# Threshold attention and a gelu feed-forward on one core: a planner whose ranks go down to single pairs and single weight pieces

## Chip, cores and metric

The kernel runs on one core of a Trainium2 chip. The metric is the device time of one execution in microseconds (us). The times given are medians of several runs.

## The reference

Two blocks follow each other. All arrays are fp32; q, k and v are 8 batches x 8 heads x 576 rows x 64, x is 4608 x 512, w_in is 512 x 2048 and w_out is 2048 x 512.

```python
def _attn_ref(q, k, v, tau):
    scale = 1.0 / np.sqrt(q.shape[-1])
    scores = scale * np.matmul(q, k.transpose(0, 1, 3, 2))
    thresh = np.max(scores, axis=-1, keepdims=True) - tau
    scores = np.where(scores >= thresh, scores, -1000000000.0)
    scores = scores - np.max(scores, axis=-1, keepdims=True)
    attn = np.exp(scores)
    attn = attn / (np.sum(attn, axis=-1, keepdims=True) + 1e-09)
    return np.matmul(attn, v)

# x = attention output, transposed to (batch * seq, heads * head_dim)
def _moe_ref(x, w_in, w_out):
    h = x @ w_in
    g = h * (1.0 / (1.0 + np.exp(-1.702 * h)))
    return g @ w_out
```

The host hands the weights over as 64-bit floats; the kernel turns them into fp32 itself.

## The kernel before

**Work.** Two heads of one batch are a *pair*: 32 pairs, four for each batch. Pairs 0 to 3 are one batch, and every four pairs complete 576 rows of x. The feed-forward block works on blocks of 256 rows; the first two blocks are computed together as soon as x of pairs 0 to 3 stands.

**One pair.** SP loads q, k and v. VectorE transposes q and k (`prep`, L522). TensorE multiplies 64x64 tiles (`scores`, L538), nine key tiles j for each pair, four matmuls each. ScalarE copies each result to SBUF (`keep`, L555); VectorE takes maxima in groups (`in_groups`, L561), over tiles (`over_tiles`, L570) and over halves (`over_halves`, L581 and L594). The maxima are transposed (`turn_rows`, L605), written to memory by SP (`row_out`, L651) and read back spread over the partitions (`row_in`, L660); pair 2 does this with a VectorE transpose instead (`spread_max`, L642). VectorE subtracts (`sub`, L666), five tiles t for each pair; ScalarE masks (`mask`, L672) and takes exponentials (`exps`, L676). TensorE multiplies by v (`values`, L687, tile pv). The sums of exponentials come from TensorE for pairs 0 to 4 (`sums_by_pe`, also L687, tile den, then `one_row`, L718 and L722, and `spread_sums`, L770 and L772), and from VectorE and a round trip through memory from pair 5 on (`turn_sums`, L744 to L749, `sums_out`, `sums_in`). `place_x` (L789) scales pv and writes it to xT.

**Weights.** There are 32 pieces, 16 of w_in and 16 of w_out. POOL issues two DMAs for each (`load_w`, L473 and L474), each piece after the one before it and when its slot is free: pieces go to one of four stages inside w_out or to one of two spare slots of the arena. A piece is converted by VectorE (`cv_ex` L484, `cv_frac` L498 and L502, `cv_end` L510) and ScalarE (`cv_power`, L492). `cv_end` frees the slot.

**Feed-forward.** For the first two blocks 16 hidden tiles are computed (`mm1_0`, L844, eight matmuls each), then tanh on ScalarE (L813) and a product on VectorE (`gelu_0`, L850), then the second matmul (`mm2`, L826) in eight groups of two weight rows for each of four row blocks. Later blocks use L804, L816 and seven-product sums (L995); the last four use L909 too. Hidden tiles use the PSUM pool psM of two banks; scores, pv and some others use psA of three slots.

**Order.** Nothing is ordered by the loops themselves. Each step becomes a *task* with an engine, a cost, a rank, the tasks that it comes after and the buffers that it takes and gives back. `run_in_order` then plays the tasks through an event loop: whenever an engine is free, the ready task with the lowest rank starts, and its instructions are issued. The program that runs on the chip holds each engine's instructions in the order so found. The rank of an attention task is the number of its pair plus a bias by kind of task:

```python
        if 0 <= rank < LAST:
            biases = EARLY if a[0] < NPAIR else SECOND if a[0] < 2 * NPAIR else LATER
            rank += CV[f.__name__] if f.__name__ in CV else biases.get(f.__name__, 0.0)
```

EARLY holds for pairs 0 to 3, SECOND for 4 to 7, LATER from 8 on, CV for the weight tasks. `W_RANK` gives six numbers from which the base rank of each weight piece is interpolated. Feed-forward matmuls have rank 1000 and most of their followers rank -9.

Of the kernel before, what the change touches and what calls it, by code (L numbers as in the profile page):

```python
# [30 lines left out]
def kernel(  # L31
# [97 lines left out]
    for x in ("raw0", "raw1", "qkT0", "qkT1", "mb"):  # L129
# [3 lines left out]


    EARLY = {
        "exps": -17.61,
        "in_groups": 12.77,
        "keep": 26.48,
        "load_qk": 6.42,
        "load_v": 0.46,  # L140
        "mask": 4.73,
        "one_group": -15.86,
        "one_row": -9.06,
        "over_halves": -11.42,
        "over_tiles": -0.06,
        "place_x": -9.61,
        "prep": -11.56,
        "row_in": 31.26,
        "row_out": -12.68,
        "scores_run": 26.41,  # L150
        "spread_max": 4.27,
        "spread_sums": 4.87,
        "sub": 8.56,
        "sums_by_pe": -5.69,
        "sums_in": 2.27,
        "sums_out": 16.51,
        "turn_rows": -16.86,
        "turn_sums": -5.4,
        "values": 24.67,
        "w_sum": 2.1,  # L160
        "x_sum": -20.63,
    }
    SECOND = {
        "exps": -12.92,
        "in_groups": 29.73,
        "keep": 6.19,
        "load_qk": 1.9,
        "load_v": 13.07,
        "mask": 1.29,
        "one_group": 2.55,  # L170
        "one_row": -2.79,
        "over_halves": -24.79,
        "over_tiles": 9.26,
        "place_x": -19.31,
        "prep": -22.42,
        "row_in": -9.56,
        "row_out": -26.33,
        "scores_run": 2.45,
        "spread_max": 6.39,
        "spread_sums": -1.67,  # L180
        "sub": 27.62,
        "sums_by_pe": 38.88,
        "sums_in": 16.9,
        "sums_out": 8.98,
        "turn_rows": 12.04,
        "turn_sums": -0.33,
        "values": 2.02,
        "w_sum": -3.88,
        "x_sum": -12.22,
    }  # L190
    LATER = {
        "exps": 1.49,
        "in_groups": 1.97,
        "keep": -9.78,
        "load_qk": -5.98,
        "load_v": -3.59,
        "mask": 21.95,
        "one_group": 4.78,
        "one_row": -20.84,
        "over_halves": 8.94,  # L200
        "over_tiles": -3.1,
        "place_x": 4.68,
        "prep": -7.1,
        "row_in": 2.23,
        "row_out": -2.52,
        "scores_run": -13.43,
        "spread_max": -3.68,
        "spread_sums": -27.9,
        "sub": 9.4,
        "sums_by_pe": 4.28,  # L210
        "sums_in": 8.55,
        "sums_out": -0.12,
        "turn_rows": -4.72,
        "turn_sums": 8.12,
        "values": 0.63,
        "w_sum": 21.55,
        "x_sum": 7.65,
    }
    CV = {
        "cv_end": -26.29,  # L220
        "cv_ex": 6.34,
        "cv_frac": -13.49,
        "cv_power": -9.91,
        "load_w": 3.03,
    }

    LAG = {"PE": 0.26, "DVE": 0.18, "ACT": 0.22, "POOL": 0.18, "SP": 0.1}
# [4 lines left out]
    def task(engine, cost, rank, f, *a, after=(), take=(), give=(), lag=None):  # L232
        if lag is None:
            lag = LAG[engine]
        if 0 <= rank < LAST:
            biases = EARLY if a[0] < NPAIR else SECOND if a[0] < 2 * NPAIR else LATER
            rank += CV[f.__name__] if f.__name__ in CV else biases.get(f.__name__, 0.0)
        tasks.append((engine, cost, rank, f, a, [x for x in after if x is not None],
                      take, give, lag))
        return len(tasks) - 1  # L240
# [9 lines left out]
    def transfer(by, time, a, kind=0, give=(), lag=1.7):  # L250
        return task(by, time, FIRST, moved, kind, after=[a], give=give, lag=lag)
# [144 lines left out]
    def own(n, *pools):  # L396
        return tuple(x + "_apart" for x in pools) if n in APART else pools
# [678 lines left out]
    FFU = 1.727  # L1076
    T_RANK = FIRST

    W_RANK = (0, 15.75, 22.55, 26.06, 2.06, 16.74)
    ready_w, w_loads, w64 = [], [], 0  # L1080
    for i in range(len(pieces)):
        y = 0 if i < NDC else 2 if i < n_in else 4
        n = NDC if i < NDC else n_in - NDC if i < n_in else n_in
        first = (0, 0, NDC, 0, n_in)[y]
        rank = W_RANK[y] + (W_RANK[y + 1] - W_RANK[y]) * (i - first) / n
        if not wide:
            ready_w.append(task("POOL", 1.2, rank, load_w, i, lag=2.5))
            continue
        x = stage(i)
        place = (f"w64_{w64 % 2}",) if x is None else (f"stage{x}",)  # L1090
        w64 += x is None
        a = task("POOL", 1.1, rank, load_w, i, after=w_loads[-1:], take=place)
        w_loads.append(a)
        a = transfer("DMW", 3.4, a)
        e = task("DVE", 0.34, rank, cv_ex, i, after=[a])
        m = task("ACT", 0.67, rank, cv_power, i, after=[e])
        a = task("DVE", 0.95 + SHARED, rank, cv_frac, i, after=[e])

        over = [ready_w[y] for y in range(i) if i >= n_in and stage(y) == (i - n_in) // PER_STAGE]
        ready_w.append(task("DVE", 0.61 + SHARED, rank, cv_end, i, after=[a, m] + over, give=place))  # L1100
# [191 lines left out]
    for n in range(NP):  # L1292
# [39 lines left out]
        if n >= JOINT:  # L1332

            a = None
            for t in range(NKT + 1):
# [11 lines left out]
                a = w  # L1347
                for j in js:
# [6 lines left out]
                    a = w  # L1355
                if t == NKT:
                    valued(m, w)
        else:
            for js in [range(x, x + 3) for x in range(0, NK, 3)] if n >= WHOLE else [[x] for x in range(NK)]:
                new = sum((own(n, "s_m") if x < NK - 1 else ("s_t",) for x in js if x % 2 == 0), ())  # L1360
                a = task(
                    "PE", 0.484 * slow * len(js), r, scores_run, n, js, after=[pq, pk] + after,
                    take=("psA",) * len(js) + new,
                    give=own(n, "qkT0", "qkT1") if js[-1] == NK - 1 and n not in TWICE else (),
                )
# [3 lines left out]
        a = task("DVE", 0.47, r, over_tiles, n, ALU.max, after=mx)  # L1369
        quick = n in BY_DMA or n in TWICE  # L1370
        a = task(
            "DVE", 1.05 if not quick else 1.3 if n in TWICE else 0.8, r, over_halves, n,
            after=[a, tau_done], take=("row",) if quick else (),
        )
        if n in TWICE:
            m = task("DVE", 0.6, r, row_blocks, n, after=[a], take=own(n, "mb"), give=("row",))
        elif n in BY_DMA:
            a = task("DVE", 0.21, r, turn_rows, n, after=[a])
            a = transfer("DMS", 0.3, task("SP", 0.65, r, row_out, n, after=[a]))
# [6 lines left out]
        for t in range(NKT + 1):  # L1386
            tail = t == NKT
            if n in TWICE:
                for j in range(2 * t, min(2 * t + 2, NK)):
# [4 lines left out]
                    a = task("ACT", 0.62, r, mask_one, n, j, after=[m] + mx, give=("psA",))  # L1394
# [3 lines left out]
            a = task(  # L1398
                "POOL" if pool else "DVE", (1.45 if pool else 0.68) if tail else 2.7 if pool else 1.3,
                r, sub, n, t, after=[y for y, x in subs if tail or x in (None, pool)],  # L1400
                give=own(n, "mb") if tail else (),
            )
            subs.append((a, pool))
            a = task("ACT", 0.7 if tail else 1.18, r, mask, n, t, after=[a])
# [4 lines left out]
        if n < NPAIR:  # L1409
# [15 lines left out]
            if n in SUMS_BY_PE:  # L1425
                a = task("DVE", 1.07, r, one_row, n, after=[den], give=("psM", "psM"))
            else:
                back += (v_m,)
        else:
# [3 lines left out]
            if n in SUMS_BY_PE:  # L1433
                a = task("PE", 4.36, r, sums_by_pe, n, every, False, after=ws + [pv], take=("psA",), give=back)
                if pv is None:
                    su = [a]
                a = task("DVE", 1.07, r, one_row, n, after=[a], give=("psA",))
        if n not in SUMS_BY_PE:
# [4 lines left out]
            a = task("DVE", 0.47, r, over_tiles, n, ALU.add, after=su + [pv], give=back)  # L1443
            if n in SUMS_BY_DMA:
                a = task("DVE", 1.46, r, turn_sums, n, after=[a], take=("row_s",))
                a = transfer("DMS", 0.3, task("SP", 0.65, r, sums_out, n, after=[a]))
                a = task("SP", 1.2, r, sums_in, n, after=[a], take=("rc",))
                summed[n] = transfer("DMS", 0.7, a, 1, give=("row_s",))
            else:
                a = task("DVE", 1.6, r, one_group, n, after=[a])  # L1450
# [41 lines left out]
```

## Time and profile before

| | |
|---|---|
| median of 3 runs | 1313.1 us (1312.97, 1313.1, 1314.63) |
| profiled execution, its own time | 1311.6 us |
| its span, first to last instruction | 1309.8 us |
| TensorE (PE) matmul busy | 1260.5 us, 96% |
| VectorE (DVE) busy | 1002.2 us, 77% |
| ScalarE (ACT) busy | 646.6 us, 49% |
| GpSimd (POOL) busy | 246.1 us, 19% |
| mean granted TensorE clock | 0.989 |

The profile is one execution, and its times are counted from the start of the span. In a row of the timeline the columns are start, length, engine, line, operation, what is written from what, and in brackets the idle time of the engine ahead of it and what ended that idle time. A row of the waits reads: who waited, for whom, us in total, number of times, longest. One fp32 matmul appears as two records, so the eight matmuls of a hidden tile are sixteen records. "PEld" is the loading of weights into TensorE.

### The profile page before, as it was taken

How to read it: one execution, taken by the hardware profiler on the slowest of the kernel's cores; microseconds unless marked ns; L12 is line 12 of the kernel's file. 1: busy time of each engine (PE TensorE's matmuls, PEld its weight loads, DVE VectorE, ACT ScalarE, POOL GpSimd, SP SyncE). 2: the span in 40 equal slices, each digit the busy share in tenths (PEclk: the TensorE clock that was granted, in tenths of full speed). 3: DMA queues.
4: the chain of work that ended last, by engine and by line, in shares of the span. 5: the costliest groups of instructions: out<-in, count | busy, mean ns of one | idle time of the engine just before them, and what ended most of it. 6: DMA issues, size and time to landing. Idle time of an engine off the chain costs nothing. (4 is left out here: it accounts for less than half of the span.)

```text
span 1309.8 us, 22824 instructions
## 1 busy us (share of the span) xinstructions
PE 1260.5 (96%) x9128; PEld 972.6 (74%) x9128; DVE 1002.2 (77%) x1601; ACT 646.6 (49%) x830; POOL 246.1 (19%) x300
## 2 busy tenths in 40 slices
PE   5869999999999999999999999999999999999998
PEld 2436854477688777777778888777777778888887
DVE  7999998989998877778877877777888864652642
ACT  5975656766664544455554545454556540210210
POOL 1301210022030212112020302020212117120120
PEclk8989999999999999999999999999999999999999
DMA  6976967264322222221222222222122110000000
GB/s 118 339 186 214 282 209 132 67 125 83 82 57 71 55 64 64 56 57 44 63 47 61 55 71 55 72 56 70 42 52 54 38 44 9 9 1 33 1 1 32
DMA packets 194309, 103.78 MB, mean 79 GB/s; under 512 B 160284, under 2 KB 171292, under 8 KB 194204
## 3 DMA queue, kind: packets, MB, share of 16 engines
q1 hardware_dynamic: 180476, 64.30, 20.6%
q0 software_dynamic: 11360, 37.74, 9.7%
q8 instruction: 71, 1.16, 0.4%
q10 hardware_dynamic: 2368, 0.30, 0.2%
q14 instruction: 34, 0.28, 0.1%
HBM read 88.40 MB, written 9.70 MB: 75 GB/s over the span
## 5 line engine op out<-in xcount | busy, mean ns | idle before, releaser
L561 DVE TRANSPOSE_TENSOR_REDUCE part<-arena 128x36 f32<-128x1152 f32 x295 | 361.5, 1241 | 45.9 <-ACT arena L555 32.3
L804 PE MATMUL hps<-xT,w_in 128*128 128x256 f32 x1536 | 336.9, 380 | 0.4 <-DVE arena L816 0.4
L804 PEld LDWEIGHTS hps<-xT,w_in 128*128 128x128 f32 x1536 | 290.8, 190 | 45.5 <-issue 5.7
L672 ACT ACTIVATE arena<-arena 128x1152 f32<-128x1152 f32 (+1 forms) x160 | 169.4, 1058 | 144.9 <-DVE arena L666 144.6
L555 ACT COPY arena<-ps 128x576 f32<-128x576 f32 x288 | 170.4, 647 | 121.2 <-PE ps L538 120.9
L666 DVE TENSOR_TENSOR arena<-arena 128x1152 f32<-128x1152 f32 (+1 forms) x158 | 197.5, 1281 | 19.6 <-DMA arena<-row 19.5
L995 PE MATMUL ops<-w_out,arena 128*128 128x256 f32 x896 | 202.9, 381 | 1.2 <-DVE arena L816 1.1
L676 ACT ACTIVATE arena<-arena,shift,scl 128x1152 f32<-128x1152 f32 (+1 forms) x160 | 200.1, 1251 | 4.1
L538 PE MATMUL ps<-arena 64*64 64x288 f32 x2304 | 174.1, 419 | 25.1 <-DVE arena L522 14.4
L995 PEld LDWEIGHTS ops<-w_out,arena 128*128 128x128 f32 x896 | 169.0, 190 | 29.1 <-DVE arena L816 3.7
L961 POOL TENSOR_TENSOR arena<-arena 128x256 f32<-128x256 f32 x56 | 50.8, 907 | 658.4 <-DVE arena L816 556.7
L687 PE MATMUL pv<-arena 64*64 64x288 f32 x2176 | 161.2, 410 | 0.0
L538 PEld LDWEIGHTS ps<-arena 64*64 64x64 f32 x2304 | 83.7, 137 | 93.6 <-ACT arena L555 30.7
L995 PE MATMUL ops<-arena 128*128 128x256 f32 x672 | 150.6, 380 | 0.0
L813 ACT ACTIVATE th<-hps 128x512 f32<-128x512 f32 x112 | 66.0, 589 | 167.9 <-PE hps L804 148.2
L995 PEld LDWEIGHTS ops<-arena 128*128 128x128 f32 x672 | 127.3, 190 | 19.3 <-issue 2.2
L687 PEld LDWEIGHTS pv<-arena 64*64 64x64 f32 x2176 | 82.0, 135 | 55.3 <-issue 12.8
L1017 DVE SCALAR_TENSOR_TENSOR osb<-ops,osb 128x256 f32<-128x256 f32 x98 | 39.5, 414 | 91.8 <-PE ops L995 85.0
L816 DVE SCALAR_TENSOR_TENSOR arena<-th,hps 128x512 f32<-128x512 f32 x96 | 64.1, 667 | 37.1 <-ACT th L813 37.0
L844 PE MATMUL hps<-xT,w_in 128*128 128x256 f32 x256 | 57.3, 382 | 1.3 <-DVE arena L850 1.2
L826 PE MATMUL ops<-w_out,arena 128*128 128x512 f32 x128 | 56.4, 596 | 0.0
L844 PEld LDWEIGHTS hps<-xT,w_in 128*128 128x128 f32 x256 | 48.1, 190 | 11.0 <-DVE arena L850 3.0
(117 smaller groups left out, 1027.8 us busy)
## 6 DMA issues: line engine op xcount, KB each, us to landing
arena<-in_v_dram SPq DMA_DIRECT2D x128, 144.0 KB
arena<-in_q_dram SPq DMA_DIRECT2D x128, 72.0 KB
out_dram<-osb SPq DMA_DIRECT2D x36, 256.0 KB
arena<-in_k_dram SPq DMA_DIRECT2D x124, 72.0 KB
arena<-row SPq DMA_DIRECT2D x62, 144.0 KB
arena<-row_s SPq DMA_DIRECT2D x54, 144.0 KB
w_out<-in_moe_w_in_dram POOLq DMA_DIRECT2D x12, 512.0 KB, 9.4
arena<-in_moe_w_out_dram POOLq DMA_DIRECT2D x12, 512.0 KB, 5.9
```

Of the source, the lines that this page charges most:

```text
L538: nc.tensor.matmul(ps[ts(c, KT), h, 0:SH], lhsT=mats[n, 1][ts(h, D), ts(j, KT)], rhs=mats[n, 0][ts(h, D), ts(c, SH)], start=True, stop=True,)
L555: nc.scalar.copy(out=sT[n, t][:, u], in_=pss.pop((n, j))[:, :, 0:SH])
L561: nc.vector.tensor_reduce(out=stats[n, op][:, t * 2 * QB : min(2 * t + 2, NK) * QB], in_=sT[n, t].rearrange("p u h (g d) -> p (u h g) d", ...
L666: engine.tensor_tensor(out=s, in0=s, in1=mbs[n].unsqueeze(1).to_broadcast(list(s.shape)), op=ALU.subtract)
L672: nc.scalar.activation(out=s, in_=s, func=AF.Prelu, alpha=STEEP)
L676: nc.scalar.activation(out=s, in_=s, func=AF.Exp, scale=scl, bias=shift)
L687: nc.tensor.matmul(o[c][ts(h, D), 0:SH], lhsT=left(j, h)[ts(c, KT)], rhs=sT[n, t][ts(c, KT), u, h, :], start=(j == 0), stop=(j == NK - 1),)
L804: nc.tensor.matmul(hidden[j][:, ts(f, BLK)], lhsT=w_in[:, c, ds((f * HF + j) * P, P)], rhs=xTs[blk][:, c, :], start=(c == 0), stop=(c == N ...
L813: nc.scalar.activation(out=ths[j], in_=hidden[j], func=AF.Tanh, scale=GELU_SCALE / 2)
L816: nc.vector.scalar_tensor_tensor(out=g[:, :, j, :], in0=two(ths.pop(j)), scalar=1.0, in1=two(hidden.pop(j)), op0=ALU.add, op1=ALU.mult,)
L844: nc.tensor.matmul(hidden[j][:, ts(i, BLK)], lhsT=w_in[:, c, ts(j, P)], rhs=xTs[i][:, c, :], start=(c == 0), stop=(c == NDC - 1),)
L995: nc.tensor.matmul(banks[blk][k][:, ts(o, HM)], lhsT=left[:, j, :], rhs=right[:, j, :], start=(j == 0), stop=(j == HF - 1),)
```

## The change

A table FINE is added: for each kind of task, a number for single pairs (0 to 11) or, for the weight tasks, single pieces (0 to 31). It is added to the rank on top of the bias by kind. All numbers of EARLY, SECOND, LATER, CV and W_RANK that have an effect are replaced as well. Costs, buffers, task lists and everything that a task computes are the same. Lines behind the table stand 31 to 32 further down in the changed file; this document uses the line numbers of the kernel before.

```diff
     EARLY = {
-        "exps": -17.61,
-        "in_groups": 12.77,
-        "keep": 26.48,
-        "load_qk": 6.42,
...
+        "exps": -15.19,
+        "in_groups": 17.23,
+        "keep": 16.21,
+        "load_qk": 18.68,
...
+    FINE = {
+        "cv_end": {0: -4.24, 1: 0.97, 2: -0.08, 3: 0.15, 4: -0.51, 5: -1.84, 6: 3.35, 7: -7.43, 9: -1.14,
...
+        "exps": {0: -2.59, 1: -0.69, 2: 6.36, 4: -3.4, 5: -2.14, 6: -1.95, 7: -3.02, 8: 0.63, 11: 0.04},
...
+        "scores_run": {1: 3.05, 2: -2.01, 3: -0.82, 4: 0.23, 6: 0.66, 7: -1.37, 8: -0.72, 9: -1.56, 11: -0.25},
...
+        "w_sum": {0: 3.24, 1: 2.7, 3: -1.58},
+    }
     CV = {
-        "cv_end": -26.29,
-        "cv_ex": 6.34,
-        "cv_frac": -13.49,
-        "cv_power": -9.91,
-        "load_w": 3.03,
+        "cv_end": -25.54,
+        "cv_ex": -1.8,
+        "cv_frac": 3.09,
+        "cv_power": -11.15,
+        "load_w": 15.66,
     }
...
             rank += CV[f.__name__] if f.__name__ in CV else biases.get(f.__name__, 0.0)
+            rank += FINE.get(f.__name__, {}).get(a[0], 0.0)
...
-    W_RANK = (0, 15.75, 22.55, 26.06, 2.06, 16.74)
+    W_RANK = (5.06, 3.62, 24.06, 7.16, 8.62, 12.37)
```

In the built program this moves instructions on TensorE, VectorE, ScalarE and SP. Up to the first feed-forward matmul, TensorE's list changes as follows: the score matmuls of pair 3 stand between the den and pv matmuls of pair 1 instead of behind them; those of pair 4 between the den and pv matmuls of pair 2; those of pair 5 between the den and pv matmuls of pair 3, with one tile of nine left behind them. In the list of L826, a run of 4 and 16 matmuls around the scores of pair 6 becomes 10 and 2, and the run between pair 5's and pair 6's `values` grows from 30 to 38. On VectorE, 10 weight pieces instead of 13 stand ahead of `place_x` of pair 3, in the order 0, 1, 2, 3, 9, 8, 6, 4, 5, 7 instead of ascending. On SP, half of the first v loads move behind the q and k loads that followed them.

## The prediction

> **What bounds the kernel now.** I read the page's totals first, then busy time by stretch, then TensorE's waits, then the timeline at the places that the waits name.
>
> ```profile
> PE 1260.5 (96%) x9128; PEld 972.6 (74%) x9128; DVE 1002.2 (77%) x1601; ACT 646.6 (49%) x830; POOL 246.1 (19%) x300
> ```
>
> The 96% is a mean over unlike stages. Stretches cut where the work changes (columns: stretch, length, then busy us of PE, PEld, DVE, ACT, POOL, granted clock, DMA share, GB/s):
>
> ```profile
> 20.00:114.00 94.00, 65.17 (x865) 36.07 (x865) 90.86 (x157) 74.52 (x90) 18.16 (x33) 0.87 0.78 231
> 114.00:165.00 51.00, 49.74 (x228) 42.14 (x230) 48.26 (x77) 27.33 (x36) 12.64 (x23) 1.00 0.79 252
> 165.00:246.00 81.00, 78.52 (x545) 40.11 (x544) 74.45 (x121) 54.52 (x64) 8.40 (x12) 1.00 0.64 153
> 246.00:420.00 174.00, 171.37 (x1328) 126.48 (x1329) 157.11 (x238) 104.83 (x134) 32.68 (x30) 0.99 0.38 82
> 420.00:1310.00 890.00, 884.59 (x6026) 723.10 (x6024) 620.14 (x991) 374.57 (x490) 171.47 (x184) 1.00 0.18 45
> ```
>
> Up to 114 us VectorE is full (90.86 of 94) and PE is not (65.17). From 114 to 246 both are nearly full. After 420 PE alone is full and VectorE has 270 us to spare. So the change, which reorders the first twelve pairs, can only save PE idle time ahead of about 420 us. PE's waits in the whole run:
>
> ```profile
> PE den L687 <- ACT arena L676: 16.5, 4, 6.8
> PE ps L538 <- DVE arena L522: 14.4, 3, 8.7
> PE ps L538 <- ACT arena L555: 6.4, 10, 2.4
> PE ps L538 <- DVE xT L789: 4.1, 3, 1.6
> PE hps L844 <- DVE arena L850: 1.2, 3, 0.8
> ```
>
> The first four are nearly all ahead of the first feed-forward matmul (L844, at 113.93). What is left after it: 1.2 on the gelus (L850), 4.9 of the 6.4 on score copies (L555), 1.5 on L816. Three places in the timeline of PE carry the argument:
>
> ```profile
> 110.27 3.73 PE L538 MATMUL ps<-arena 64*64 64x288 f32 x32 [1.64 <-DVE xT L789]
> ...
> 157.83 7.17 PE L844 MATMUL hps<-xT,w_in 128*128 128x256 f32 x32 [0.79 <-DVE arena L850]
> ...
> 246.30 1.43 PE L538 MATMUL ps<-arena 64*64 64x288 f32 x16 [2.44 <-ACT arena L555]
> ```
>
> Ahead of the third, on VectorE:
>
> ```profile
> 220.62 1.36 DVE L666 TENSOR_TENSOR arena<-arena 128x1152 f32<-128x1152 f32 x1 [0.91 <-DMA arena<-row]
> 224.23 0.78 DVE L522 STREAM_TRANSPOSE arena<-arena 128x576 f32<-128x576 f32 x1 [2.25 <-DMA arena<-in_q_dram]
> ```
>
> The `sub` of pair 6 starts at 220.62. ScalarE's chain of masks and exps for pairs 6 and 7 hangs on it and runs, with one hole of 1.72 us caused by that q transfer, until 245.63; only then does it copy the first scores of pair 8, for which PE sits 2.44 us.
>
> [...]pair 3's `one_row` ran at 104.75, then four weight conversions (L510) stood between it and its reciprocal at 108.08, and PE waited for what followed. [...]The row of maxima goes out to memory and back, two in series; in the trace it took 6 to 9 us from its transpose (L605) to the `sub` that waited for it (285.87 to 292.11; 263.07 to 272.50), so the measured pair is used.
>
> **The change, step by step.** Only ranks change. Both built programs hold the same 4565 matmuls, 64x64 and 128x128 forms alternate equally often (63 switches), and no DMA is added. What changes is place in the queues. I add up VectorE work from start-to-start times of the trace: reduction L561 1.29, `sub` 1.27, one weight piece 2.0 (L484 0.34, L498 0.46, L502 0.61, L510 0.61), `one_row` to `place_x` 3.0.
>
> *A, up to the first L844.* Ahead of `place_x` of pair 3, VectorE now does 10 weight pieces for 13 (-6.0) and 19 reductions for 16 (+3.9): -2.1 us. VectorE idles under 1 us from 19 to 109, so this moves its end from 110.1 to 108.0. Against it: from pair 3's transpose of maxima to its first `sub` there is now 6.7 us of other work (two conversions 3.4, pair 2's `one_row` to `place_x` 3.0, one L484 0.3), where the round trip takes 6 to 9. I take 0.6 of idle, bounds 0 and 2.5: 108.7. Pair 5's score matmuls now stand between pair 3's den/pv matmuls, so one score remains after them where 16 matmuls (3.73 us) ran between `place_x` and L844. First L844 at 108.9 for 113.93: **5.0 us earlier**. Pair 1's exps end later (its copies of pair 3's scores are interleaved; some 64 for 57), which only psM and psA slots feel.
>
> *B, the 14 hidden tiles.* Each is 8 matmuls, 3.45 us; with two banks tile j waits for gelu j-2. From the end of `place_x` of pair 3 to the end of gelu 11 VectorE has 46.5 us of work in the new order, 46.6 in the old; the old trace took 50.1, so 3.5 is idle, mostly for weights. The three postponed pieces are all paid here. Gelu 11 ends at 108.7 + 50.0 = 158.7, tile 13 runs to 162.3, where pv of pair 4 begins (164.93 before). PE, ready 5 us early, waits for gelus about 3.6 us instead of 1.2. **Lead left: 2.6 us.**
>
> *C, the second matmuls.* PE's list from pv of pair 4 to the seventh weight group of L826 adds to 31.7 us: it arrives at 194.0. That group needs the 30th piece, whose conversion comes 82.4 us of VectorE work after `place_x`; with the 4.9 us of idle that the old trace had to this point, 196.0. **Lead left: 0.6.** PE then runs 47.4 us, through the rest of L826, pv of pair 5 and pv of pair 6 up to its second tile, and stands at the 246.30 wait at about 243.4.
>
> *D, that wait.* Up to the first `sub` of pair 6 VectorE executes exactly the same instructions in both orders (206.4 us by my durations), so its start cannot move except by idle time. I take 220.8 for 220.62: the row leaves 1.5 us later and SP sends it back directly, 8 us. The second `sub` now follows at once and the q transpose comes third, so of ScalarE's 1.72 us hole nothing need remain: first copy at 244.2 for 245.63, PE on at 244.9 for 246.30. **-1.4 us.**
>
> *E, afterwards.* Pairs 8 to 11 are reordered too, but VectorE's instruction sets meet again at pair 12. PE's waits there sum to 3.7; I leave them, bounds -1.5 and +1.5.
>
> Sum: -1.4. The profiled execution took 1311.6 (span 1309.8) and would take 1310.2; it lies 1.5 under the median of the three runs, 1313.1, so the forecast is 1313.1 - 1.4 = **1311.7**. A measurement of this kernel tells a change from none at about 0.2%, 2.6 us.
>
> **The rivals.** *Faster: VectorE's idle shrinks.* Its waits for weights up to 188 us are 0.82, 1.41 and 1.51, its wait for pair 6's row 0.91: 4.65 in all. If the later demand finds weights landed, C's wait of 2.0 goes and the 220.8 comes up to 3.5 earlier. For it: POOL's loads in the old order were held by conversions, not by bandwidth. Against: slots are freed later too. With two thirds of it, -1.4 - 3.1: 1308.6.
>
> *Slower: pieces 10 to 15 land late.* Pieces 4 and 5 hold the two spare slots of the arena and are now converted eighth and ninth, at about 98 and 100. Pieces 10 and 11 need those slots, and every later load is chained behind them. Before, 10 was issued at 61.12, 11 at 89.16, 14 and 15 at 104.43 and 106.65; now six go out between 98 and 106. At 2.8 us each (1.05 MB at the 372 GB/s of 40 to 60 us) they land from 107 to 121, just when VectorE asks (109 to 122). At the 4.2 us of 14 and 15 (104.43 to 112.76), the last lands at 128 and VectorE, in order, holds gelus behind it: 5 to 6 us that nothing downstream gives back. It decides from about 3.1 us a piece. -1.4 + 5.5: 1317.2. The row of A at 2.5 would add 1.9.
>
> That nothing moves is excluded: the built orders differ from the first interleaved score on.
>
> **How the numbers follow.** Forecast case 0.50, alone 1309.3 to 1314.4 (the row's 0 to 2.5, E's 1.5 each way); faster rival 0.26; slower rival 0.24. Faster than 1310.5 takes 0.25 of the faster rival and 0.08 of the forecast's edge: 0.33; slower than 1315.7 takes 0.23 of the last and 0.01: 0.24; between, 0.43. The range, 1307.5 to 1316.8, takes the centre of the faster rival and part of the slower.
>
> **What would show it.** Right: first L844 near 109; gelu waits (L844 <- L850) of 3 to 4 us for 1.2; a new wait of L826 for a converted piece near 194 to 196; the wait of L538 on L555 near 245 still there; VectorE's first `sub` of pair 6 within 1.5 us of 220.6. Wrong: that `sub` before 218, or no wait near 245 (then faster); VectorE waiting on weight DMA for over 3 us between 108 and 130 (then slower); a first L844 after 112.

## The result, and the profile after

The kernel after takes 1319.27 us in the median of five runs (1317.92 to 1322.6), the kernel before 1312.97 on the same chip: ratio 1.0053, 95% interval 1.0039 to 1.0067. **It is slower by about 7 us** by the ratio (0.53% of 1313; the medians lie 6.3 apart), outside the forecast's range. The profiled execution of after took 1321.6 us, span 1319.8, which is 10.0 more than before's span. The two profiles lie further apart than the medians, since before's lies 1.4 below its median and after's 2.3 above.

Line numbers in rows of the changed kernel are 31 or 32 higher than those used so far: L570 is L538 (scores), L836 is L804, L848 is L816, L858 is L826, L876 is L844, L882 is L850, L698 is L666 (`sub`), L554 is L522 (`prep`). In kernels of the experiments they stand another 10 to 50 higher than in the kernel that the experiment starts from.

The totals of the page, and busy time by stretch (columns as before: stretch, length, PE, PEld, DVE, ACT, POOL, granted clock, DMA share, GB/s):

```profile
PE 1264.2 (96%) x9128; PEld 974.6 (74%) x9128; DVE 1002.3 (76%) x1601; ACT 647.1 (49%) x830; POOL 247.3 (19%) x300
```

```profile
20.00:114.00 94.00, 69.61 (x891) 39.33 (x888) 88.87 (x146) 74.60 (x91) 18.15 (x33) 0.85 0.67 197
114.00:165.00 51.00, 48.85 (x247) 40.49 (x249) 50.14 (x89) 27.58 (x36) 10.16 (x18) 1.00 0.85 257
165.00:246.00 81.00, 77.17 (x516) 38.49 (x508) 69.42 (x109) 49.16 (x59) 10.82 (x16) 1.00 0.77 185
246.00:420.00 174.00, 162.77 (x1282) 119.03 (x1283) 156.52 (x242) 106.31 (x135) 30.15 (x30) 0.97 0.35 76
```

The new order leaves VectorE's work as it was, 1002.3 us in all for 1002.2. Up to 114 us PE does 4.4 us more than before, as the interleaved scores promised. From 165 to 246 VectorE does 5.0 less, and from 246 to 420 PE does 8.6 less. So the loss lies between 165 and 420. PE's waits name the places:

```profile
PE ps L570 <- ACT arena L587: 9.3, 5, 6.8
...
PE hps L836 <- DVE arena L848: 3.6, 2, 3.3
...
PE hps L876 <- DVE arena L882: 1.9, 3, 0.8
PE ops L858 <- DVE w_out L542: 1.6, 1, 1.6
```

The wait for score copies has one instance of 6.8 us where before had 2.4. The wait of L836 for a gelu (3.3) is new. In PE's timeline:

```profile
110.26 1.56 PE L876 MATMUL hps<-xT,w_in 128*128 128x256 f32 x6
112.10 5.88 PE L876 MATMUL hps<-xT,w_in 128*128 128x256 f32 x26 [0.28 <-DVE xT L821]
...
198.71 1.12 PE L858 MATMUL ops<-w_out,arena 128*128 128x512 f32 x2 [1.57 <-DVE w_out L542]
...
252.59 2.20 PE L570 MATMUL ps<-arena 64*64 64x288 f32 x16 [6.79 <-ACT arena L587]
...
313.19 8.86 PE L836 MATMUL hps<-xT,w_in 128*128 128x256 f32 x32 [3.33 <-DVE arena L848]
321.89 7.07 PE L1027 MATMUL ops<-w_out,arena 128*128 128x256 f32 x32
```

The row at 252.59 is the "gate", the first scores of pair 8: 252.59 for 246.30, **6.3 us late**. The row at 313.19 holds two losses: 3.33 us of waiting, and 32 matmul records that take 8.86 us where 32 of the same form took 7.17 in before (the row at 157.83): 1.7 us at a lower granted clock, 0.81 from 313.19 to 322.05 for 1.00 in before's row. Together 5.0; before lost 1.4 in this part (0.44 on a gelu at 287.97, 0.95 on a score copy at 327.88). 6.3 + 5.0 - 1.4 = 9.9, the 10.0 of the spans. That is an account of where PE stood or ran slowly, not yet of causes. For the 1.7 it would mislead: the row at 321.89 uses the next gelu, and where the 32 records took 7.17 (kernels 1, 4 and 8 and hybrid H2 below) PE waited 1.35 us for that gelu at this point. By that estimate the lower clock costs about 0.2 here (8.70 us from row to row, 8.53 in those kernels); the rest would have been waiting.

What VectorE did ahead of both places:

```profile
214.75 0.21 DVE L637 STREAM_TRANSPOSE flat<-flat 128x32 f32<-128x32 f32 x1
...
224.36 2.63 DVE L698 TENSOR_TENSOR arena<-arena 128x1152 f32<-128x1152 f32 x2 [1.93 <-DMA arena<-row]
...
233.88 0.78 DVE L554 STREAM_TRANSPOSE arena<-arena 128x576 f32<-128x576 f32 x1 [4.97 <-DMA arena<-in_k_dram]
...
309.26 1.36 DVE L698 TENSOR_TENSOR arena<-arena 128x1152 f32<-128x1152 f32 x1 [5.53 <-DMA arena<-row]
...
312.49 0.65 DVE L848 SCALAR_TENSOR_TENSOR arena<-th,hps 128x512 f32<-128x512 f32 x1
```

The first row is the transpose of pair 6's maxima, the second pair 6's first `sub`: 3.7 us later than before's 220.62. The third is the transpose of pair 8's k: it waits 4.97 us for its transfer, and behind it on VectorE stand the last two `sub` of pair 6, which start at 234.59, and those of pair 7, from 240.30 on. ScalarE's masks, with the exponentials behind them, wait 2.29 and 1.73 us for these. The last two rows explain 313: pair 9's first `sub` waits 5.53 us for its row, and the gelu that PE needs stands behind it.

### The profile page after: what moved, and what is told of

Read it like the earlier page. It is cut to its first block, busy times and chain, and to the rows that moved or that the text cites. A ratio compares the mean times of both kernels' runs of the same rounds, so it can differ in the third digit from the quotient of the medians.

```text
span 1319.8 us, 22820 instructions
## 1 busy us (share of the span) xinstructions
PE 1264.2 (96%) x9128; PEld 974.6 (74%) x9128; DVE 1002.3 (76%) x1601; ACT 647.1 (49%) x830; POOL 247.3 (19%) x300
## 5 line engine op out<-in xcount | busy, mean ns | idle before, releaser
L593 DVE TRANSPOSE_TENSOR_REDUCE part<-arena 128x36 f32<-128x1152 f32 (+1 forms) x295 | 360.0, 1241 | 50.7 <-ACT arena L587 37.6
L836 PE MATMUL hps<-xT,w_in 128*128 128x256 f32 x1536 | 339.0, 381 | 3.6 <-DVE arena L848 3.6
L836 PEld LDWEIGHTS hps<-xT,w_in 128*128 128x128 f32 x1536 | 291.8, 191 | 49.8 <-issue 5.7
L698 DVE TENSOR_TENSOR arena<-arena 128x1152 f32<-128x1152 f32 (+1 forms) x158 | 197.4, 1278 | 22.8 <-DMA arena<-row 22.6
L570 PE MATMUL ps<-arena 64*64 64x288 f32 x2304 | 176.0, 421 | 25.9 <-ACT arena L587 9.3
L570 PEld LDWEIGHTS ps<-arena 64*64 64x64 f32 x2304 | 85.6, 138 | 92.2 <-ACT arena L587 29.1
L848 DVE SCALAR_TENSOR_TENSOR arena<-th,hps 128x512 f32<-128x512 f32 x96 | 64.1, 667 | 36.3 <-ACT th L845 36.2
L876 PE MATMUL hps<-xT,w_in 128*128 128x256 f32 x256 | 57.8, 383 | 2.4 <-DVE arena L882 1.9
L858 PE MATMUL ops<-w_out,arena 128*128 128x512 f32 x128 | 56.7, 597 | 1.6 <-DVE w_out L542 1.6
L876 PEld LDWEIGHTS hps<-xT,w_in 128*128 128x128 f32 x256 | 47.8, 190 | 12.5 <-DVE arena L882 4.4
```

The costliest lines, as they stand in the source:

```text
L570: nc.tensor.matmul(ps[ts(c, KT), h, 0:SH], lhsT=mats[n, 1][ts(h, D), ts(j, KT)], rhs=mats[n, 0][ts(h, D), ts(c, SH)], start=True, stop=True,)
L593: nc.vector.tensor_reduce(out=stats[n, op][:, t * 2 * QB : min(2 * t + 2, NK) * QB], in_=sT[n, t].rearrange("p u h (g d) -> p (u h g) d", ...
L698: engine.tensor_tensor(out=s, in0=s, in1=mbs[n].unsqueeze(1).to_broadcast(list(s.shape)), op=ALU.subtract)
L836: nc.tensor.matmul(hidden[j][:, ts(f, BLK)], lhsT=w_in[:, c, ds((f * HF + j) * P, P)], rhs=xTs[blk][:, c, :], start=(c == 0), stop=(c == N ...
L876: nc.tensor.matmul(hidden[j][:, ts(i, BLK)], lhsT=w_in[:, c, ts(j, P)], rhs=xTs[i][:, c, :], start=(c == 0), stop=(c == NDC - 1),)
```

## The experiments

In the experiments the planner's order is kept in a list instead of being issued at once; single tasks are then moved in that list, each to the place behind a named one, and the list is issued. Nothing else changes.

```diff
-                tasks[i][3](*tasks[i][4])
+                order.append(i)
...
+        for f, a, g, b in MOVES:
+            x = order.pop(place(f, a))
+            order.insert(place(g, b) + 1, x)
+        for i in order:
+            tasks[i][3](*tasks[i][4])
```

All ratios are to the kernel before on the same chip, with 95% intervals; a difference of two ratios is given in us by way of 1313 us. The times of events come from one profiled execution of each kernel. These vary: pair 6's first `sub` starts between 222.8 and 225.5 in the eight kernels that have after's order on VectorE up to it, and between 220.5 and 221.5 in the four that have before's. The theory: the loss has two places, the gate (k of pair 8 late, row of pair 6 late) and the gelu behind pair 9's `sub`. Rivals: the weights come late; SP's queue is what delays k; the places overlap, so that mending one only lengthens the other.

**1. k's transposes later.**

```diff
+    MOVES = (("prep", (8, 1), "in_groups", (6, 2, ALU.add)),)
```

> The changed kernel's order, with one VectorE instruction moved: pair 8's transpose of k (prep, L522) goes from between the third and fourth sub of pair 6 to behind pair 6's first three sums. Theory 1: the wait for the k transfer (4.97 us in the changed kernel, VectorE in order, four subs behind it) sits on the chain sub, mask, exps of pairs 6 and 7 that ends in PE's 6.79 us wait for a score copy. Then ScalarE's two holes of 2.29 and 1.73 us close, the PE wait falls to about 2.8 us, and the median comes down by about 4 us, to 1315. Rival, the extra time comes from pairs 8 and later: the wait at 252 us shrinks but PE waits as much more later, and the median stays at 1319 within 1.

Measured 1.0032 (1.0023 to 1.0042), 2.8 us off after; the two intervals just overlap. The wait on k is gone (its transpose runs at 236.07 without one) and the gate comes at 251.04 with a wait of 4.33 us, more than expected: pair 7's first `sub` now waits 1.93 us for its row. Part of the gain went into the next wait.

**2. Pair 9's first sub behind the gelu.**

```diff
+    MOVES = (("sub", (9, 0), "place_x", (8,)), ("mask", (9, 0), "over_tiles", (10, ALU.max)),
+             ("exps", (9, 0), "mask", (9, 0)), ("in_groups", (9, 0, ALU.add), "sub", (9, 1)))
```

> The changed kernel's order, with pair 9's first sub, its mask and its exps moved from ahead of a gelu (L816) and its tanh to behind the next ones. In the changed kernel this sub waits 5.53 us for pair 9's row of maxima, the gelu stands behind it on VectorE, and PE waits 3.33 us for the gelu at 313 us. Theory 1: that wait goes to under 0.5 us and the median falls by about 3.3 us, to 1316. Rival, VectorE is behind anyway at this point: the wait moves to a later gelu or score copy within 60 us, and the median falls by under 1 us.

Measured 1.0018 (1.0011 to 1.0025): 4.6 us off after, more than the 3.3 of the wait. The wait at 313 is gone, and so is the lower clock that followed it: from 300 to 330 the granted clock was 1.00, 0.94 in after. A smaller wait for the next gelu takes its place, as the rival had it, but it takes back only a part:

```profile
318.88 7.17 PE L1040 MATMUL ops<-w_out,arena 128*128 128x256 f32 x32 [1.36 <-DVE arena L861]
```

That row starts 3.0 us earlier than in after (321.89), and the gate is 0.7 later (253.28, wait 6.84): 3.7 us gained in the profiles. The intervals of the two ratios leave room for 3.7 as for 4.6.

**3. Both.**

> Both moves of e1 and e2 together. Theory 1: the two waits are independent and the gains add: about -7.3 us from 1319.3, so 1312, level with the kernel before. Rival: the second wait depends on how late PE comes to it after the first; PE then arrives 4 us earlier at an unchanged row transfer, the waits trade, and the pair gains no more than the larger single move, 1315.

Measured 0.9999 (0.999 to 1.0009): 7.1 us off after where the single moves gave 2.8 and 4.6. The gains add, and after's order with these two moves is level with before.

**4. What makes k late: the weight sum `t_plus`.** `t_plus` is an accumulating transfer of 1 MB that POOL issues (L955 before, L987 after). It adds one quarter of w_out to the negative of another, for the later seven-product sums; the recorded texts call it the residual addition. Of four of them the second is issued ahead of pair 8's q loads in before, and beside its k loads in after; its issue on POOL in before, then in after:

```profile
212.33 1.57 POOL L955 DMA_DIRECT2D arena<-w_out  x1 [11.10 <-ACT arena L951]
```

```profile
223.41 1.57 POOL L987 DMA_DIRECT2D arena<-w_out  x1 [10.44 <-ACT arena L983]
```

In this run it and its two negations on ScalarE (L951) are issued behind pair 7's `sub`s.

```diff
+    MOVES = (("t_minus", (1, 0), "sub", (7, 4)), ("t_minus", (1, 1), "t_minus", (1, 0)),
+             ("t_plus", (1,), "t_minus", (1, 1)))
```

> The changed kernel's order, with the second 1 MB accumulating DMA (the second of L955, on POOL's queue, and its two ScalarE negations L951) moved behind pair 7's subs, out of the time in which pair 8's k is loaded. Theory 1 (collision): in the changed kernel this DMA is issued at 223.41, 0.6 us ahead of the k loads at 223.97, and delays them; without it k lands 2.5 to 4 us sooner, VectorE's wait of 4.97 us falls under 2.5, and the median falls by 2.5 to 4 us. Rival (SP's queue): the k loads are late because SP issues the row, q and k in order after a late row; the wait for k stays within 1 us of 4.97 and the median within 1 us of 1319.3.

Measured 1.0021 (1.0013 to 1.0028): 4.2 us off after, the gate at 248.94 with 3.36. Of the 3.65 us that the gate gains in the profiles, 1.2 are an earlier `sub` of pair 6 (223.20), which the move doesn't explain: the order up to it is the same. No VectorE instruction waits for k any more, though the order of SP's queue and of VectorE is untouched. SP's issue of the q and k loads in after, then in this run:

```profile
221.73 2.20 SPq L442 DMA_DIRECT2D arena<-in_q_dram  x4
223.97 3.88 SPq L442 DMA_DIRECT2D arena<-in_k_dram  x4
```

```profile
220.72 2.20 SPq L454 DMA_DIRECT2D arena<-in_q_dram  x4
222.96 2.73 SPq L454 DMA_DIRECT2D arena<-in_k_dram  x4
```

Next to the addition even the issue of k takes 1.15 us longer, and VectorE gets the data 6 us after the issue ends (227.85 to 233.88); in this run it takes k 2 us after it (225.69 to 227.68), without a wait.

**5. The same move on the kernel before.**

> The kernel before, with the second residual addition (t_plus and its two negations) moved behind pair 7's subs, as was done to the kernel after. Collision theory: the 1 MB accumulate transfer slows whatever is loaded next to it; in the order of before it is issued at 212.33, just ahead of the q and k loads of pair 8 (q: issue of four transfers took 6.05 us), so the wait of 2.25 on q at 224.23 shrinks below 0.5, ScalarE's hole of 1.72 goes, and the gate of 246.30 comes 1.5 to 2.3 us earlier: ratio to before about 0.9985. Rival (the q loads are slow in this order because of the weight loads still under way): the 2.25 stays and the ratio is 1.000. Where the addition goes later, its own result is stored later; nothing on PE needs it, so no cost is expected.

Measured 0.9987 (0.9978 to 0.9996). The wait of 2.25 on q is gone (VectorE transposes q at 222.78, right behind the first `sub`), and SP issues the four q transfers in 2.20 us instead of 6.05. **This is the one version whose interval lies below before's time**, by 1.7 us (0.5 to 2.9). But the gate did not come earlier, as the theory wanted:

```profile
237.94 1.99 ACT L963 ACTIVATE arena<-arena 128x1024 f32<-128x1024 f32 x2
...
247.09 2.20 PE L550 MATMUL ps<-arena 64*64 64x288 f32 x16 [2.80 <-ACT arena L567]
```

The first row is the two negations. They moved too, out of ScalarE's idle time ahead of the `sub` into the chain of masks and exps, and cost there about what the hole of 1.72 had cost. From the first mask of pair 6 to the first copy of pair 8 that chain took 23.6 us in before (222.01 to 245.63) and 23.5 here (222.89 to 246.42). So the wait is explained, but where the 1.7 us come from is not shown.

**6. The addition moved into after's place, in the kernel before.**

> The kernel before, with one thing of after alone: the second residual addition is issued behind the second sub of pair 6, as in after, instead of ahead of the q loads of pair 8. Collision theory: the transfer now runs beside the k loads; the wait of 2.25 on q at 224 goes and one of 4 to 5 us on k takes its place, the gate comes 2 to 3 us later than 246.3, ratio 1.0015 to 1.0025. Rival, that in after k was late because q, k and both rows share SP's queue with the row of pair 7: k no later than q was, ratio 1.000.

Measured 1.0014 (1.0005 to 1.0023). One moved transfer makes after's wait, on VectorE of this kernel:

```profile
229.36 0.78 DVE L534 STREAM_TRANSPOSE arena<-arena 128x576 f32<-128x576 f32 x1 [4.77 <-DMA arena<-in_k_dram]
```

The gate waits 4.54 us, at 249.47. POOL issues the addition at 218.82, SP the k loads from 218.57 on; the negations run at 216.51, in ScalarE's idle time. With 4 and 5 the collision is shown from both sides: taken away the wait goes, put in it comes. ScalarE's chain from the first mask of pair 6 to the first copy of pair 8 gives its size. It took 26.2 us in after and 26.1 here, and 23.7 in 4, although 4 has the negations (2.0 us) inside the chain and the other two don't. So 4 and 5 understate what the transfer alone costs. Why the loads land late beside it (the transfer engines, or SP's issue, which was slow for k in after, 3.88 us, and for v here, 5.33) is not shown.

**7. The last two moves together, and all three.**

> The kernel after with two moves: pair 9's first sub behind the gelu (no wait of 3.33 at 313) and the second residual addition behind pair 7's subs (no wait on k at 234). If the two losses are separate, the gains add: about -4.6 and -4.2 us against after, ratio to before 0.9985 to 0.999. If PE's lead lost at the gate is partly what the later wait would have absorbed, less is gained: ratio 1.000 to 1.001.

> As the last, and the k transposes of pair 8 behind pair 6's sums as well. With the addition out of the way k is there when it is asked for, so moving its transposes saves only their 1.5 us ahead of the last subs of pair 6; ScalarE's chain gains at most that. Theory that ScalarE's chain from the first sub to the first copy of pair 8 sets the gate: gate 0 to 1.5 us earlier than in the last kernel, ratio 0.9975 to 0.999. Rival, that row(7) becomes the wait again: no gain, the same ratio as the last kernel, and sub(7,0) waits for its row.

Measured 0.9997 (0.9989 to 1.0006) and 0.9993 (0.9982 to 1.0005). The two moves take back all of the loss within the interval, 7.4 us. That is less than 4.6 + 4.2 = 8.8, but the intervals don't tell these apart. With the addition out of the way no effect of the k transposes is seen: the two kernels can't be told apart, and from pair 6's first `sub` to the gate both take 25.7 us. The gate itself is still late with the two moves, at 249.91, 3.6 after before's, because pair 6's first `sub` is (224.17). What that costs in the end is too small for these intervals.

**8. Where the later start of pair 6 comes from.** First, three short weight instructions fill two early waits.

```diff
+    MOVES = (("cv_ex", (8,), "sub", (2, 0)), ("cv_ex", (7,), "cv_ex", (8,)),
+             ("cv_ex", (4,), "cv_ex", (5,)))
```

> The kernel after with three of the short weight instructions (the exponent step of pieces 8, 7 and 4) moved ahead of the two early waits that after has and before has not: 1.05 us at 68.29 (one_row of pair 1 waits for its sums) and 0.41 at 90.85 (the first sub of pair 3 waits for its row). Theory that VectorE's own queue sets the time up to the first sub of pair 6: the end of place_x of pair 3 comes 1.0 to 1.4 us earlier (112.49 to about 111.3), the first sub of pair 6 and the gate 0.5 to 1.4 earlier, ratio to before 1.0042 to 1.0049. Rival, that weights arriving late set it: the end of place_x moves, the waits on w_out pieces at 166 to 171 grow by as much, and the gate and the ratio (1.0053) stay.

Measured 1.0039 (1.0026 to 1.0053), which overlaps after's own interval. Counted from pair 0's first `sub` (32.04 here, 31.59 in after), `place_x` of pair 3 begins 0.7 us earlier; pair 6's first `sub` is at 223.35, the gate at 251.88. Inconclusive as to time; of the 1.46 us removed, half was left by `place_x` of pair 3, and a `sub` at 223.35 lies within what after's own order gives (222.8 to 225.5).

**9. Hybrids.** The planners of both kernels number the same tasks alike, and after 684 tasks both have issued the same set. A hybrid issues a HEAD, copied from one kernel's order, and then the rest in the other's order. They are lettered H1 to H6.

```diff
+        first = set(HEAD)
+        for i in list(HEAD) + [i for i in order if i not in first]:
+            tasks[i][3](*tasks[i][4])
```

> A hybrid: the first 684 tasks of the program's order (up to the subs of pair 6, by which point both kernels have issued the same set) as in the kernel after, all that follows as in the kernel before. Theory that after's loss has two separate places: the wait of L538 on the copies of pair 8 stands as in after (about 252.5, 6.8 us), and no wait on a gelu of more than 1.4 us follows; ratio to before 1.002 to 1.003. Rival, that a tail takes back what a late head loses (PE arrives later at the tail's own waits): ratio 1.000 to 1.001. Rival, that the head alone is responsible for all of it: 1.005.

> The other hybrid: the first 684 tasks as in the kernel before, all that follows as in the kernel after. Theory of two places: the wait at pair 8 is that of before (near 246.3, 2.4 us), and the wait on the gelu behind the first sub of pair 9 (3.3 us in after) comes about 6 us earlier, near 307, at 3 us or more; ratio to before 1.002 to 1.003. Rival, that after's tail is only slow because it starts late: no wait there, ratio 1.000.

Measured 1.0026 (1.0017 to 1.0036) for after's head (H1), 1.0022 (1.0016 to 1.0029) for after's tail (H2): 1.0048 together, about after's 1.0053. H1 has the gate at 252.57 with a wait of 7.48, and no wait on a gelu of more than 0.5 behind it. **Two separate losses of like size.** H2 on PE:

```profile
246.18 1.40 PE L619 MATMUL ps<-arena 64*64 64x288 f32 x16 [2.49 <-ACT arena L636]
...
306.88 7.17 PE L885 MATMUL hps<-xT,w_in 128*128 128x256 f32 x32 [3.45 <-DVE arena L897]
315.41 7.17 PE L1076 MATMUL ops<-w_out,arena 128*128 128x256 f32 x32 [1.35 <-DVE arena L897]
```

The gate is before's, and the wait on the gelu is there at 3.45: it belongs to the tail's order, not to a late start. This time 7.17 follows it, with no loss of clock (1.00 from 300 to 330), and then a wait of 1.35 for the next gelu.

> The first 560 tasks (up to pair 5's fourth sub and the 15th gelu: all that steps A and B of the prediction speak of, and the weight loads) as in the kernel after, the rest as in the kernel before, the second residual addition and the q and k loads of pair 8 included. Theory that the weights and small waits of the early part cost 1 to 2.7 us of VectorE's time and the placing of the addition the rest: first sub of pair 6 at 222 to 223.3, the wait on q at about 2.3 as in before, the gate at 248 to 249, ratio 1.001 to 1.002. Rival, that the early part costs nothing and the middle all (as steps A to C of the prediction would have it): sub at 220.6, ratio 0.999 to 1.000.

H3 measured 1.0032 (1.0021 to 1.0044), more than either theory said. The joint made a wait of its own: PE stood 5.52 us at 192.47 for score copies, as ScalarE stood behind weight conversions whose pieces had not landed (3.01 us ahead of the one at 191.15; VectorE waited 1.50, 0.88, 0.98 and 0.88 us for pieces from 190 to 200). `sub` of pair 6 came at 225.75. The head loads its weights as late as after does, and the rest asks for them as early as before does.

> The first 404 tasks (up to the fourth gelu, about 125 us) as in the kernel before, the rest as in the kernel after. At this cut the two programs differ only by piece 16, three reductions and a few tasks around one gelu, so the joint itself should cost little. Theory that the small waits of after's first 112 us (weights 1.4, sums of pair 1 1.05, row of pair 3 0.41) make the first sub of pair 6 late: it comes 1.5 to 2.5 us earlier than after's 224.4, the gate at 250 to 251, the k wait (5) and the wait behind pair 9's sub (3.3) stay; ratio 1.0032 to 1.0042. Rival, that the stretch from 404 to 684 (weights of the second half, row of pair 6) makes it late: sub and gate as in after, ratio 1.0053.

H4 measured 1.0058 (1.0046 to 1.007): the rival's time, although the `sub` came early as in the theory. `place_x` of pair 3 came at 109.59, 2 us ahead of after's, but nothing of it is left in the time. Pair 6 on VectorE, then PE:

```profile
212.38 0.21 DVE L669 STREAM_TRANSPOSE flat<-flat 128x32 f32<-128x32 f32 x1
...
222.38 2.63 DVE L730 TENSOR_TENSOR arena<-arena 128x1152 f32<-128x1152 f32 x2 [2.32 <-DMA arena<-row]
```

```profile
251.31 2.20 PE L602 MATMUL ps<-arena 64*64 64x288 f32 x16 [7.88 <-ACT arena L619]
312.86 10.02 PE L868 MATMUL hps<-xT,w_in 128*128 128x256 f32 x32 [3.15 <-DVE arena L880]
```

The `sub` came 2.0 us earlier than in after, the gate 1.3, and the matmuls at 312.86 only 0.3. In between PE ran at a lower clock for longer (0.55 from 246 to 256, 0.67 in after): from the gate to the next L826 (here L890) took 8.90 us, 7.77 in after. Then the 32 records took 10.02 us, at clocks of 0.50, 0.50 and 0.89 in the three stretches of 3 us from 312 on.

> The reverse: the first 404 tasks as in the kernel after, the rest as in the kernel before. Theory of the early waits: first sub of pair 6 at 222 to 223 for 220.6, gate at 247.5 to 248.5, no wait near 307 to 313, ratio 1.001 to 1.002. Rival, that the early part is harmless: sub within 0.5 of 220.6, ratio 1.000.

H5 measured 1.0035 (1.0023 to 1.0047), a miss for both theories. Again before's order asked for weights too early: POOL issued the first of w_out at 129.40, as after's head has it (130.93 in after, 120.05 in before), VectorE waited 7.0 us in seven pieces from 133 to 152, PE 9.33 us on a gelu at 141.60. So this cut, like that of H3, tells nothing of the early waits themselves.

> e13 with the two moves that helped after: the second residual addition behind pair 7's subs, and pair 9's first sub behind the gelu. If the three losses of after (early waits, addition beside the k loads, sub ahead of the gelu) are separate and complete, what is left is at or ahead of the kernel before: ratio 0.9975 to 0.999, gate at 246 to 247. Rival, that they overlap (an earlier gate only lengthens a later wait): ratio 0.9995 as in the kernel with the two moves alone.

H6 measured 1.0008 (1.0 to 1.0016): no better than the two moves alone (0.9997), where the theory had 0.9975 to 0.999. Its `sub` of pair 6 came at 224.51 and its gate at 250.25, although its order up to the `sub` is that of H4, which had 222.38. So one execution differs from the next by as much as the early waits are worth. In the time they are no third cause of a size that these runs resolve; whether they make the `sub` late is open.

## Why the prediction was wrong, step by step

*A, the first L844.* Forecast 108.9, measured 110.26: three of the first tile's matmuls ran ahead of pair 3's x, and the fourth waited for it until 112.10. `place_x` of pair 3 ended at 112.49 for a forecast 108.7. Of the 3.8, 0.6 is a later start of the execution (pair 0's first `sub` at 31.59 for 30.98); 1.2 are weight pieces 0 and 1, for which VectorE waited 0.82 and 0.58 (before 0.22); 1.05 is `one_row` of pair 1, asked for before TensorE had its sums. The row of pair 3 cost 0.41 where I took 0.6. That leaves about 1.1 unresolved. The term that was mis-sized is the idle time of VectorE's early queue, taken to stay as it was.

*B, the hidden tiles.* Forecast: gelu waits of 3.6, end of the tiles 162.3. Measured: 1.9, and the last row of L876 ends at 163.0 (141.92 + 21.09). With three matmuls already done at 112.10, PE was about 1.9 us behind the forecast there, and it waited 1.7 less: little of A's miss was left, 0.7 at the end of the tiles.

*C, the second matmuls.* Forecast a wait of 2.0 at 194 to 196 for a converted piece; measured 1.57, ending at 198.71. Right in kind, 2.7 late.

*D, the gate: the main step that failed.* It said that the first `sub` of pair 6 "cannot move except by idle time", and let that idle time grow by 0.2 us. It grew by 3.7. The `sub` is not released by VectorE; it waits for a row. The row's trip starts at the transpose of the maxima. In before that row of VectorE's timeline is

```profile
211.19 0.21 DVE L605 STREAM_TRANSPOSE flat<-flat 128x32 f32<-128x32 f32 x1
```

In after it stands at 214.75, 3.6 later. I had taken 1.5. The work ahead of it is indeed 1.6 us more (195.3 us busy for 193.7), but the idle time ahead of it is 1.95 more, and that I had left out. From there to the `sub` it took 9.4 us in before (220.62), in after 9.6 (224.36), in H4 10.0. I had taken 8, less than before's own trip of this row. The two terms, 2.1 and 1.6 short, make up the 3.6 between the forecast 220.8 and 224.36. VectorE was ready at 222.43.

The second failure is in the next sentence, that of ScalarE's hole "nothing need remain". The order also moves `t_plus`, which the step does not mention: its transfer beside the k loads was put at nothing. The hole for q (2.25) went, but one for k came (4.97), with two more `sub`s of pair 6 behind it. Experiments 4 to 6 show this cost: 4.2 us in after, and 3.5 between two places of the transfer in before's order (0.9987 and 1.0014). What the later `sub` alone costs was not isolated. The gate was forecast at 244.9 and came at 252.59.

*E, afterwards.* "I leave them, bounds -1.5 and +1.5" for PE's waits after the gate. They rose by 3.6: 3.33 and 1.7 of clock at 313, less the 1.4 of before. This is the other step that failed. Pairs 8 to 11 had been said to be reordered, and nothing was worked out on what stood behind a waiting `sub`: pair 9's first stood ahead of a gelu, and moving it took 4.6 us off after (experiment 2).

*The rivals.* The faster one did not come: VectorE's waits for weights ahead of pair 6 sum to 4.4 (before 4.0), and the row's wait went from 0.91 to 1.93. The slower rival had the sign and nearly the time (1317.2), but by luck: its mechanism is another. Its premise was right: pieces 10 to 15 were issued from 102.30 on, after 44.2 us of idle on POOL. But VectorE's timeline has no wait for a w_in transfer after 100 us, for VectorE's list asked for them later too. H3 and H5, where late loads meet a list that asks early, measured 1.0032 and 1.0035.

*The bounds.* Those given for the forecast case, 1309.3 to 1314.4, are not the sum of their parts: 0.6 less or 1.9 more for the row and 1.5 each way for E give 1309.6 to 1315.1.

*Signs named ahead.* "Wrong: a first L844 after 112" was just not met (110.26, its fourth matmul at 112.10). Of the signs for right, the new wait of L826 and the wait at the gate came, the gelu waits were too short (1.9), and the `sub` was out by 3.7 where 1.5 was allowed. The `sub` was the sign that told of the miss.

## What to carry to other kernels

For an instruction that waits on a transfer, follow the transfer's start, not the sum of work ahead of it: the trip of pair 6's row started 3.6 us later here, and 1.95 of these were idle time. And take the length of the trip from the same row in the kernel before (9.4 us there, 9.6 in after). When a planner moves a large transfer, look at which small load it now runs beside, and at what stands behind that load in the list of the engine that waits for it (here seven `sub`s behind a wait of 4.97 us). And when a tuned order is mended, mend the waits that end last: two moves took back all of the loss here, while an early part that ran 2 us ahead of after's gave nothing that could be measured. A task that is moved takes its helpers along: in experiment 5 the two negations cost in their new place about what moving `t_plus` had saved.

## What the hardware showed that was not expected

Around some of its waits TensorE was granted a lower clock, down to 0.50 at the gate of after. The granted clock (after the busy time of PE) was, in after and then in before:

```profile
249.00:252.00 3.00, 0.00 (x0) 0.56 0.01 2
252.00:255.00 3.00, 2.40 (x20) 0.50 0.28 98
255.00:258.00 3.00, 3.00 (x44) 0.80 0.00 0
...
315.00:318.00 3.00, 3.00 (x9) 0.56 0.14 45
```

```profile
246.00:249.00 3.00, 2.70 (x32) 0.71 0.29 98
249.00:252.00 3.00, 3.00 (x44) 0.72 0.00 0
252.00:255.00 3.00, 3.00 (x38) 1.00 0.06 11
```

Before's wait of 2.4 us was followed by clocks of 0.71 and 0.72, after's of 3.3 by 0.56, after's of 6.8 by 0.50 and 0.80, with 0.56 while PE still stood. From the gate to the next L826 PE took 7.74 us in before and 7.77 in after; the same matmuls one pair later took 5.95 in both. So 1.8 us were lost at the gate whether it waited 2.4 or 6.8, and the clock is no part of the difference there. It isn't regular: over all the kernels of this document that stretch took from 6.67 (H5, after a wait of 2.60) to 8.90 (H4, 7.88). Away from the gate, a wait of 3.45 (H2) was followed by full clock, 1.00, one of 3.15 (H4) by clocks of 0.50 to 0.89 and a loss of 2.9, part of it time in which PE would have waited for the next gelu anyway. What decides is open; it was not tried.

The other surprise is how far one accumulating transfer of 1 MB reaches: where it was issued beside k loads of four transfers, VectorE waited 4.5 to 5.1 us for k in five kernels (4.97 in after, 5.09 in kernel 2, 4.77 in kernel 6, 5.05 in H1, 4.52 in H4), and where it was issued ahead of the q loads, in before, 2.25 us for q.
